# A convolution and a gated layer on one core: each half of a product, copy and sum placed by itself

## Chip, core and metric

The kernel runs on one core of a Trainium2 chip. The metric is the device time of one execution in microseconds (us), the median of several runs. All data are float32; the weights of the layer come as float64 and are turned into float32 by the kernel itself.

## What is computed

A lightweight convolution (each of 8 groups of 24 channels has 7 taps, made by a softmax), then a layer with a sigmoid gate:

```python
# x (8, 4096, 192), weight (8, 7), w_in (192, 2048), w_out (2048, 192)
w = softmax(weight, axis=-1)
conv[b, s, head] = sum_k w[head, k] * x_pad[b, s + k, head]   # causal, 6 zeros ahead
h = conv.reshape(32768, 192) @ w_in
g = h * (1 / (1 + exp(-1.702 * h)))
out = g @ w_out
```

## The kernel before

**Steps.** The 32768 tokens are cut into 32 steps ("big") of 1024: 512 tokens of each of two sequences. The arrays are multiplied by schemes in the manner of Strassen: fewer products of blocks, paid with sums of blocks before and after. Step 0 is done plainly, beside the conversion of the weights; step 1 has its own order; steps 2 to 31 run through the same tables.

**First part of a step** (h = conv @ w_in, and the gate). 20 products (TERMS), each in two rounds (v = 0, 1: two halves of the hidden units), 40 in all. A product has two halves, h = 0 and 1: half 0 takes the rows 0 to 63 of TensorE's array, half 1 the rows 64 to 127, each a matmul of 64x128 weights (w_in_s) on 512 columns of the convolved input (conv_t), each into its own PSUM bank (product1, the matmul is line 598). Products add up in PSUM tiles a0 to a8; between them ScalarE copies a tile to SBUF or to another tile (copy2, L633 and L635 with a sign), VectorE adds or subtracts tiles (sum2, L639), and ScalarE makes the gelus into g (L615 from PSUM, L620 from SBUF). All results that another product adds to must be read first: product 19 adds to a4 only when a5 has been copied from it. In before, `do` issues an item for both halves at once: product half 0, half 1; copy half 0, half 1; sum half 0, half 1.

**Second part of a step** (out = g @ w_out). 78 "main" pieces and 78 "side" matmuls. A main piece is three matmuls of 128x32 weights (w_form, w_out_s) on 256 columns, one in each of three groups of 32 array columns; a side matmul takes the fourth group. `go` issues a main piece and then one side matmul, always in this turn (L855), and the copy of a finished side result (L880). VectorE joins results (L355, L357), transposes the outputs (L771), SyncE stores them. Sums of blocks of g (L355, L357 too, and the accumulating DMAs of POOL, L831) run alongside.

**What prepares the next steps.** Taps of the convolution (ScalarE, L483), their adds (POOL, L501), accumulating DMAs (POOL, L506), sums of conv_t (POOL, L355), SyncE's transfers that put blocks on the other half of the partitions ("cross", L526), loads of x and their transposes (VectorE, L438).

**What sets the order.** All engines take their instructions in the order in which the program issues them, and wait for each other by semaphores. That order is written by hand in tables: ORDER for the first part, PLAN for the second, OPENING for step 0 and step 1, with queues (`todo`, `ready`, `adds`, `tree`, `pieces`) from which "tap", "add", "vsum" and "cross" take the next piece of preparation.

Of the kernel before, what the change touches and what calls it, by code (L numbers as in the profile page):

```python
# [15 lines left out]
def kernel(  # L16
# [38 lines left out]
    xt_pool = ctx.enter_context(tc.tile_pool(name="xt", bufs=1))  # L55
# [6 lines left out]
    xts = {}  # L62
# [103 lines left out]
    def side(big, other, b):  # L166
        return cross_of(big, b) if other else slot_of(big, b)
# [20 lines left out]
    def form(i):  # L188
# [8 lines left out]
    COPY_O = [  # L197
        [(10, 2), (16, 1), (17, 0), (18, 0), (8, 7), (9, 5), (11, 3, -1), (12, 6, -1)],
        [(13, 3), (14, 3), (15, 0), (19, 4), (20, 4), (21, 5), (22, 7)],
        [],  # L200
        [(23, 1), (24, 1), (1, 14), (7, 0, -1)],
    ]
    SUMS_O = [
# [4 lines left out]
    ]  # L208
    TURN_O = (9, 17, 20, 21)

# [105 lines left out]
    def split_rest(i, part=slice(0, PIECE)):  # L316

        lo, hi, m, e = words(i, part)
        ef = e.bitcast(F32)
        act.activation(ef, e, AF.Relu, bias=bias[:, 0:1], scale=-1.0)  # L320
        act.activation(e, ef, AF.Relu, bias=bias[:, 1:2], scale=-(2.0**23))
# [43 lines left out]
    w_left = list(SUMS_W)  # L365

    def next_w(n):
        for _ in range(n):
            add_up(lambda j: w_in_s[:, j, :], *w_left.pop(0))

# [6 lines left out]
    def round_o(i):  # L377
# [15 lines left out]
        round_piece(NW + i, dsts)  # L393

    def add_forms(stage):
        for dst, src, *sign in COPY_O[stage]:
            if sign:
                act.mul(form(dst), form(src), -1.0)
            else:
                act.copy(form(dst), form(src))  # L400
        for dst, src in SUMS_O[stage]:
            nc.gpsimd.dma_start(out=form(dst), in_=form(src), accum_op=ALU.add)

    def end_forms():
        for i in TURN_O:
            act.mul(form(i), form(i), -1.0)
# [26 lines left out]

    def transpose_x(big, c, n=None):
        if big not in xts:
            xts[big] = xt_pool.tile([P, NC, 2, XT], F32, name="xt")
        ns = slice(0, 2) if n is None else slice(n, n + 1)
        vec.transpose(  # L438
            xts[big][:, c, ns, :].rearrange("p n (j t) -> p (n j) t", t=Q),
            xin[:, ns, :, :].rearrange("p n j d -> p (n j) d")[:, :, c * R : c * R + Q],  # L440
        )
# [10 lines left out]
    def tap_home(big, c, k):  # L452
        if big == 1:
            return homes_1[c][k - 1]
        if big < 3:
            return (first_taps if c == 0 else taps[3])[k - 1]
        return taps[c][k - 1]

    def conv_src(big, c, k, ns=slice(0, 2)):
        return xts[big][:, c, ns, Q - PAD + k : Q - PAD + k + T]  # L460

    def conv(big, c, k, ns=slice(0, 2), times=vec.tensor_scalar_mul):
        src = conv_src(big, c, k, ns)
        dst = own(big)[:, 2 * c + ns.start : 2 * c + ns.stop, :]
        tap = cw[:, c, k : k + 1]
        if k == 0:
            times(dst, src, tap)
# [5 lines left out]
    DMA_TAPS = (0,)  # L473
    TAPS_IN = (0, 2, 1)
    ADDS_IN = [(1, 6), (2, 5), (2, 6)] + [(c, k) for c in (2, 1) for k in range(1, K) if (c, k) not in ((1, 6), (2, 5), (2, 6))]
    TREE = {2: [(1, 2)], 4: [(3, 4)], 6: [(5, 6), (0, 1), (3, 5), (0, 3)]}
    TREE_1 = {2: {2: [(1, 2)], 4: [(3, 4), (0, 1)], 6: [(5, 6), (0, 3), (0, 5)]}, 0: {2: [(1, 2)], 4: [(3, 4)], 6: [(5, 6)]}}

    def tap(big, c, k):

        dst = own(big)[:, 2 * c : 2 * c + 2, :]
        home = tap_home(big, c, k) if k else dst
        act.mul(home, conv_src(big, c, k), cw[:, c, k : k + 1])  # L483
        if k and c not in DMA_TAPS and big > 1:
            adds.append((ADDS_IN.index((c, k)), dst, home))
            adds.sort(key=lambda a: a[0])
            if big == 2:
                next_add()
            return
        homes = [dst] + [tap_home(big, c, i) for i in range(1, K)]  # L490
        for a, b in (TREE if big > 1 else TREE_1[c]).get(k, ()):
            tree.append((homes[a], homes[b]))
        if big < 3:
            end_taps(2 if big == 2 and k == K - 1 else 0)

    tree, adds = [], []

    def next_add():
        if adds:
            _, dst, home = adds.pop(0)  # L500
            nc.gpsimd.tensor_add(dst, dst, home)  # L501

    def add_taps():
        if tree:
            out, src = tree.pop(0)
            nc.gpsimd.dma_start(out=out, in_=src, accum_op=ALU.add)  # L506

    def add_pair(c, a, b):

        dst = own(1)[:, 2 * c : 2 * c + 2, :]  # L510
        homes = [dst] + [tap_home(1, c, i) for i in range(1, K)]
        vec.tensor_add(homes[a], homes[a], homes[b])

    def end_taps(left=0):
        while len(tree) > left:
            add_taps()
# [13 lines left out]
    def copy_over(b):  # L530

        for o in range(2):
            act.copy(conv_t[halves[1 - o], cross_of(0, b), :], own(0)[halves[o], b, :])

    pieces, sums_left = [], []
    LAST_AT = {s[0]: i for i, s in enumerate(SUMS_C)}
    ENDS = (NBLK, NBLK + 3, NBLK + 6, NB - 2, NB)
    GROUPS = [range(*ends) for ends in zip(ENDS, ENDS[1:])]  # L540

    def cross_piece():
        if pieces:
            cross(*pieces.pop(0))

    def cross_blocks(big):

        bs = list(REST)
        while bs:
            n = 1  # L550
            while n < min(3, len(bs)) and bs[n] == bs[0] + n:
                n += 1
            pieces.append((big, bs[0], bs[0] + n))
            bs = bs[n:]

    def next_sum():
        if sums_left:
            big, i = sums_left.pop(0)
            sums_c(big, *SUMS_C[i])
            for b in GROUPS:  # L560
                if max(LAST_AT[s] for s in b) == i:
                    pieces.append((big, b[0], b[-1] + 1))

    def begin_sums(big):
        sums_left.extend((big, i) for i in range(len(SUMS_C)))

    def prepare(big):

        for k in range(K if big < 3 else 0):
            yield "", 0.76 if k else 0.48, lambda k=k: conv(big, 1, k)  # L570
        yield f"conv {big}", 0.0, lambda: None
        def done():
            need(f"taps {big}")
            while adds:
                next_add()
            if OPEN_SUM:
                sums_c(big, *OPEN_SUM)
            cross(big, OPEN, OPEN + 1)

        yield f"done {big}", 0.0, done  # L580

    def prepare_taps(big):

        order = [(c, k) for c in (0, 2) for k in range(K)]
        if big > 2:
            order = [(c, 0) for c in TAPS_IN] + [(c, k) for c in TAPS_IN for k in range(1, K)]
        for c, k in order:
            yield "", 1.0, lambda c=c, k=k: tap(big, c, k)
        yield f"taps {big}", 0.0, lambda: None

    def product1(slot, a, b, big, v, first=False):
# [3 lines left out]
        for h in range(2):  # L595
# [11 lines left out]
    ALL = slice(0, TOK)  # L607

    def gelu(b, u, v, src, sign=1):
# [3 lines left out]
        if isinstance(src, list):  # L613
            for h in range(2):
                act.activation(  # L615
                    dst[:, :, h, :], src[h].rearrange("p (o t) -> p o t", o=2), AF.Gelu_apprx_sigmoid,
                    scale=float(sign),
                )
        else:
            act.activation(  # L620
                dst.rearrange("p o h t -> p h o t"),
                src.rearrange("p h (o t) -> p h o t", o=2),
                AF.Gelu_apprx_sigmoid,
                scale=float(sign),
            )
# [3 lines left out]

    def copy2(dst, src, sign=1):  # L630
        for h in range(2):
            if sign == 1:
                act.copy(bank(dst, h), bank(src, h))  # L633
            else:
                act.mul(bank(dst, h), bank(src, h), -1.0)  # L635

    def sum2(op, dst, a, b):
        for h in range(2):
            op(*(bank(t, h) for t in (dst, a, b)))  # L639

# [623 lines left out]
```

## Time and profile before

| | us |
|---|---|
| median of 3 runs (2262.1 to 2263.56) | 2262.73 |
| the profiled execution | 2262.78 |
| its span, first to last instruction | 2261.1 |
| granted TensorE clock, mean | 1.000 |
| step 0 and step 1 (to the first product of step 2's first part) | up to 174.4 |
| a step from 3 on: first part, second part | 35.4, 33.9 |

In the profile's rows, PE is TensorE's matmuls, PEld its weight loads, DVE VectorE, ACT ScalarE, POOL GpSimd and SP SyncE. A row of a group or of the timeline has the line of the kernel, the engine, the operation, the tile written and those read (without numbers), shapes, and how many instructions it merges (x157). A row of the timeline starts with its start and length in us and ends in square brackets with the idle time of the engine ahead of it and what ended it. A row of the chain of waits is a stretch of the work that ended last.

### The profile page before, as it was taken

To read this page: it belongs to the slowest core of one execution; us is meant where nothing else is said; L and a number is where in the kernel's file an instruction comes from. 1 tells how busy PE (TensorE), PEld (TensorE's weight loads), DVE (VectorE), ACT (ScalarE), POOL (GpSimd) and SP (SyncE) were. 2 spreads that over 40 slices of the span, in tenths; PEclk is the share of its full clock that TensorE was granted. 3 is DMA by queue.
4 is the path that set the end of the run, shared out by engine and by line. 5 is a ranking of instruction groups with operands and counts; after the bars stand their busy time and mean duration, and the time that the engine had idled before them with its cause. 6 is when DMAs were issued, how large, how long until landed. Compare 5 with 4: busy or idle time off the path is not lost.

```text
span 2261.1 us, 62136 instructions
## 1 busy us (share of the span) xinstructions
PE 2248.2 (99%) x24966; PEld 1552.0 (69%) x24966; DVE 1985.3 (88%) x2970; ACT 1707.7 (76%) x3233; POOL 1063.9 (47%) x1098
## 2 busy tenths in 40 slices
PE   9999999999999999999999999999999999999999
PEld 5366567766777766777667776667776677766775
DVE  8998888988889888889888898888988888988888
ACT  8677877777777778777787777787777877777754
POOL 1545544455543555444555445554355544455510
PEclk9999999999999999999999999999999999999999
DMA  8986657766667666576565776666866657765543
GB/s 198 174 158 133 125 114 150 143 128 127 121 131 159 128 128 126 111 160 140 125 132 114 141 152 128 129 124 118 163 134 128 124 114 151 144 127 103 104 92 71
DMA packets 275679, 298.05 MB, mean 132 GB/s; under 512 B 119104, under 2 KB 203328, under 8 KB 275392
## 3 DMA queue, kind: packets, MB, share of 16 engines
q0 software_dynamic: 57648, 150.69, 37.0%
q1 hardware_dynamic: 216096, 142.99, 27.8%
q8 instruction: 198, 3.24, 0.6%
q14 instruction: 89, 0.73, 0.1%
q10 hardware_dynamic: 1648, 0.39, 0.1%
HBM read 53.15 MB, written 25.17 MB: 35 GB/s over the span
## 4 chain that ended last, share of the span: by engine, by line
PE 96%; DVE 2%; ACT 1%; issue 1%; DMA 1%; POOL 0%; DVEq 0%; ACTq 0%; POOLq 0%; SPq 0%
PE slot L598 49%; PE slot L855 45%; PE slot L1120 1%; DVE g L357 1%; DMA g<-osbs 0%; PE slot L1115 0%; DVE room L357 0%; ACT g L615 0%; PE slot L946 0%; DVE room L639 0%; ACT w_form L483 0%; DMA xin<-in_x_dram 0%; DVE slot L639 0%; DVE room L355 0%; DVE osbs L771 0%
## 5 line engine op out<-in xcount | busy, mean ns | idle before, releaser
L598 PE MATMUL slot<-conv_t,w_in_s 64*128 64x512 f32 x5152 | 1147.4, 594 | 3.3 <-ACT room L633 1.5
L598 PEld LDWEIGHTS slot<-conv_t,w_in_s 64*128 64x128 f32 x5152 | 663.3, 186 | 474.6 <-issue 312.1
L855 PE MATMUL slot<-g,w_form 128*32 128x256 f32 x9672 | 894.2, 379 | 0.7 <-DVE room L357 0.7
L855 PEld LDWEIGHTS slot<-g,w_form 128*32 128x32 f32 x9672 | 575.6, 110 | 128.9 <-DVE room L357 2.1
L501 POOL TENSOR_TENSOR conv_t<-conv_t,g 128x512 f32<-128x512 f32 x354 | 449.0, 1275 | 88.4 <-ACT g L483 65.4
L855 PE MATMUL slot<-g,w_out_s 128*32 128x256 f32 x5952 | 467.5, 379 | 1.3 <-DVE g L357 0.8
L357 DVE TENSOR_TENSOR g<-g 128x1024 f32<-128x1024 f32 x372 | 450.4, 1224 | 8.0 <-DMA g<-osbs 1.0
L880 ACT COPY room<-slot 32x256 f32<-32x256 f32 x651 | 237.2, 364 | 289.8 <-PE slot L855 281.5
L639 DVE TENSOR_TENSOR room<-slot,room 128x512 f32<-128x512 f32 x620 | 383.6, 679 | 67.8 <-PE slot L598 67.8
L633 ACT COPY room<-slot 128x512 f32<-128x512 f32 x620 | 337.7, 595 | 77.7 <-PE slot L598 61.7
L483 ACT ACTIVATE g<-xt,cw 128x512 f32<-128x512 f32 x534 | 353.9, 715 | 3.7
L620 ACT ACTIVATE g<-room 128x1024 f32<-128x1024 f32 x248 | 265.7, 1071 | 79.0 <-DVE room L639 49.3
L615 ACT ACTIVATE g<-slot 128x512 f32<-128x512 f32 x528 | 282.5, 610 | 51.9 <-PE slot L598 32.8
L831 POOL DMA_DIRECT2D g<-g x124 | 128.1, 1038 | 355.0 <-PE slot L855 330.8
L639 DVE TENSOR_TENSOR slot<-slot,room 128x512 f32<-128x512 f32 x372 | 239.7, 689 | 53.8 <-PE slot L598 52.2
L855 PEld LDWEIGHTS slot<-g,w_out_s 128*32 128x32 f32 x5952 | 239.7, 110 | 43.2 <-DVE room L639 23.3
L355 POOL TENSOR_TENSOR conv_t<-conv_t 128x256 f32<-128x256 f32 x210 | 179.3, 860 | 129.2 <-PE slot L598 119.6
L855 PE MATMUL slot<-osbs,w_form 128*32 128x256 f32 x2232 | 229.5, 379 | 0.0
L506 POOL DMA_DIRECT2D g<-g x120 | 105.9, 883 | 238.1 <-ACT g L483 99.4
L855 PEld LDWEIGHTS slot<-osbs,w_form 128*32 128x32 f32 x2232 | 132.5, 110 | 23.6
L639 DVE TENSOR_TENSOR slot<-room,slot 128x512 f32<-128x512 f32 x124 | 79.8, 687 | 41.8 <-PE slot L598 41.8
L855 PE MATMUL slot<-room,w_form 128*32 128x256 f32 x1488 | 112.9, 379 | 0.0
(166 smaller groups left out, 1662.6 us busy)
## 6 DMA issues: line engine op xcount, KB each, us to landing
g<-g POOLq DMA_DIRECT2D x124, 512.0 KB, 6.5
xin<-in_x_dram SPq DMA_DIRECT2D x240, 180.0 KB, 4.2
conv_t<-conv_t SPq DMA_DIRECT2D x186, 192.0 KB, 5.4
g<-g POOLq DMA_DIRECT2D x120, 256.0 KB, 5.4
conv_t<-conv_t SPq DMA_DIRECT2D x186, 128.0 KB, 2.9
out_dram<-osbs SPq DMA_DIRECT2D x186, 128.0 KB, 2.7
g<-room POOLq DMA_DIRECT2D x31, 512.0 KB, 5.1
conv_t<-g POOLq DMA_DIRECT2D x60, 256.0 KB, 5.4
```

The source lines that it names most:

```text
L355: eng.tensor_add(v(dst), v(a), v(b))
L357: eng.tensor_sub(v(dst), v(a), v(b))
L483: act.mul(home, conv_src(big, c, k), cw[:, c, k : k + 1])
L501: nc.gpsimd.tensor_add(dst, dst, home)
L598: nc.tensor.matmul(slot[h], w_in_s[halves[h], a, v * P : (v + 1) * P], src, start=first, stop=True, skip_group_check=True,)
L615: act.activation(dst[:, :, h, :], src[h].rearrange("p (o t) -> p o t", o=2), AF.Gelu_apprx_sigmoid, scale=float(sign),)
L620: act.activation(dst.rearrange("p o h t -> p h o t"), src.rearrange("p h (o t) -> p h o t", o=2), AF.Gelu_apprx_sigmoid, scale=float(sign),)
L633: act.copy(bank(dst, h), bank(src, h))
L639: op(*(bank(t, h) for t in (dst, a, b)))
L831: nc.gpsimd.dma_start(out=spot(dst), in_=spot(a), accum_op=ALU.add)
L855: nc.tensor.matmul(dst, w, t, start=first, stop=last, skip_group_check=True)
L880: act.copy(to, d)
```

## The change

The amount of work on each engine is unchanged: the same 12483 matmuls, 3230 instructions of ScalarE, 2970 of VectorE, the same DMAs; of the last step's stores one moves from ScalarE's queue to SyncE's. Only the order changes, and with it the waits (semaphore instructions: PE 727 to 582, DVE 1380 to 1344, ACT 906 to 794, POOL 660 to 543, SP 302 to 414).

- `do` takes one half of a product, copy or sum (the last entry of an item; None for both).
- ORDER, PLAN and the queues of preparation are gone. A table STEP, run for the steps 2 to 30, names each instruction or half at its place; LAST does so for step 31.
- In the second part "m" i is main piece i, "s" i side matmul i and "t" i the copy of a finished side result. They stand one by one and no longer strictly in turn; two side tiles have changed places.
- OPENING (steps 0 and 1) is written as such a table too, with the conversion of the weights (split, clip, join, sign, round) cut into its single instructions.

```diff
-    def product1(slot, a, b, big, v, first=False):
+    def product1(slot, a, b, big, v, first=False, hs=range(2)):
...
-        for h in range(2):
+        for h in hs:
...
-        def go(n):
-            for _ in range(n):
-                w, t = now["steps"].pop(0)
-                for c in range(NC):
-                    one_matmul(chunk(now["to"], c), w[:, chunk_cols(c)], t, now["first"], not now["steps"])
-                now["first"] = False
-                d, ws, ts, st, to = side.pop(0)
-                one_matmul(d, ws, ts, st, to is not False)
-                if to is not False:
-                    act.copy(to, d)
...
+        h = args[-1]
+        hs = [h] if h is not None else []
+        if kind == "prod":
+            t, dst, _ = args
+            product1(at(dst), *TERMS[t], big, v, (half, dst, h) not in begun, hs)
...
+    def main_part(i):
+        dst, w, t, first, last = now["todo"][i]
+        for c in range(NC):
+            one_matmul(chunk(dst, c), w[:, chunk_cols(c)], t, first, last)
+
+    def side_part(i):
+        d, w, t, first, to = now["aside"][i]
+        one_matmul(d, w, t, first, to is not False)
...
-    for big in range(1, N_BIG):
...
-            first_products(big, (half, begin_half(), ahead), ORDER)
...
+    for big in range(2, N_BIG - 1):
+        run(STEP, big)
```

Three places show how the order moves.

TensorE in the first part, round 0, around the products 10 and 19. Each row is one half of a product; before, an even and the next odd bank are halves 0 and 1 of one tile. Before, in pairs: products 18 (into a2, slot_73 and slot_74), 10 (a4, slot_69 and slot_70), 17 (a1), 19 (a4), 11 (a1):

```order
L598 MATMUL slot_73<-conv_t,w_in_s 128x512
L598 MATMUL slot_74<-conv_t,w_in_s 128x512
L598 MATMUL slot_69<-conv_t,w_in_s 128x512
L598 MATMUL slot_70<-conv_t,w_in_s 128x512
L598 MATMUL slot_67<-conv_t,w_in_s 128x512
L598 MATMUL slot_68<-conv_t,w_in_s 128x512
L598 MATMUL slot_69<-conv_t,w_in_s 128x512
L598 MATMUL slot_70<-conv_t,w_in_s 128x512
L598 MATMUL slot_67<-conv_t,w_in_s 128x512
L598 MATMUL slot_68<-conv_t,w_in_s 128x512
```

After: a4 is slot_66 (half 0) and slot_67 (half 1), a2 slot_70 and slot_71, a1 slot_64 and slot_65.

```order
L481 MATMUL slot_66<-conv_t,w_in_s 128x512
L481 MATMUL slot_71<-conv_t,w_in_s 128x512
L481 MATMUL slot_67<-conv_t,w_in_s 128x512
L481 MATMUL slot_70<-conv_t,w_in_s 128x512
L481 MATMUL slot_65<-conv_t,w_in_s 128x512
L481 MATMUL slot_64<-conv_t,w_in_s 128x512
L481 MATMUL slot_66<-conv_t,w_in_s 128x512
L481 MATMUL slot_67<-conv_t,w_in_s 128x512
```

Half 0 now goes 10, 18, 17, 19 and half 1 goes 18, 10, 11, 19: product 10 of half 0 stands a product earlier than that of half 1, and ScalarE's two copies a5 <- a4 follow one product apart.

TensorE at the start of the second part. "x3" is a main piece, a single row or "x2" are side matmuls. Before:

```order
L855 MATMUL slot_67<-g,w_out_s 32x256 x3
L855 MATMUL slot_68<-g,w_form 32x256
L855 MATMUL slot_67<-g,w_out_s 32x256 x3
L855 MATMUL slot_68<-g,w_form 32x256
L855 MATMUL slot_67<-g,w_out_s 32x256 x3
L855 MATMUL slot_68<-g,w_form 32x256
```

After:

```order
L741 MATMUL slot_67<-g,w_form 32x256 x2
L741 MATMUL slot_64<-g,w_out_s 32x256 x6
L741 MATMUL slot_65<-g,w_form 32x256 x2
L741 MATMUL slot_64<-g,w_out_s 32x256 x3
L741 MATMUL slot_64<-g,w_form 32x256 x3
L741 MATMUL slot_64<-g,w_out_s 32x256 x3
L741 MATMUL slot_71<-g,w_form 32x256 x2
```

Two side matmuls stand ahead of the first main pieces, and main pieces of different sums (slot_64 with w_out_s or w_form) alternate.

VectorE where step 1 begins. L639 (after: L343) with room and a slot is the sum k0 of step 1, the rows on w_in_s are sums of the weights, L771 (after: L514) turns outputs of step 0. Before:

```order
L771 STREAM_TRANSPOSE osbs<-conv_t 96x16x32
L355 TENSOR_TENSOR w_in_s<-w_in_s 128x256
L357 TENSOR_TENSOR w_in_s<-w_in_s 128x256
L1192 TENSOR_TENSOR room<-room,slot_68 96x512
L357 TENSOR_TENSOR w_in_s<-w_in_s 128x256
L771 STREAM_TRANSPOSE osbs<-slot_70 96x16x32
L771 STREAM_TRANSPOSE osbs<-room 96x16x32
L639 TENSOR_TENSOR room<-slot_73,room 128x512
L639 TENSOR_TENSOR room<-slot_74,room 128x512
```

After:

```order
L343 TENSOR_TENSOR conv_t<-conv_t 128x256 x2
L341 TENSOR_TENSOR conv_t<-conv_t 128x256
L514 STREAM_TRANSPOSE osbs<-slot_67 96x16x32
L1149 TENSOR_TENSOR room<-room,slot_65 96x512
L343 TENSOR_TENSOR room<-slot_70,room 128x512
L343 TENSOR_TENSOR room<-slot_71,room 128x512
L343 TENSOR_TENSOR slot_70<-slot_64,room 128x512
```

The last transpose (osbs<-room) and two sums of weights, which stood ahead of k0, stand behind it.

More of the change, by code (lines that the diff above doesn't have):

```diff
@@ L471, in conv, with add_tap, tree, pair @@
             )
[L473 to L477, printed above, removed]
-    def tap(big, c, k):
[L481 to L516, printed above, removed]
+    def tap(big, c, k):
+        act.mul(tap_home(big, c, k), conv_src(big, c, k), cw[:, c, k : k + 1])
+    def add_tap(big, c, k):
+        nc.gpsimd.tensor_add(tap_home(big, c, 0), tap_home(big, c, 0), tap_home(big, c, k))
+    def tree(big, c, a, b):
+        nc.gpsimd.dma_start(out=tap_home(big, c, a), in_=tap_home(big, c, b), accum_op=ALU.add)
+    def pair(big, c, a, b):
+        vec.tensor_add(tap_home(big, c, a), tap_home(big, c, a), tap_home(big, c, b))
     def sums_c(big, dst, a, op, b):
@@ L528, in cross, with copy_over @@
             )
[L530 to L589, printed above, removed]
-    def product1(slot, a, b, big, v, first=False):
+    def copy_over(b, o):
+        act.copy(conv_t[halves[1 - o], cross_of(0, b), :], own(0)[halves[o], b, :])
+    def product1(slot, a, b, big, v, first=False, hs=range(2)):
         s, c = slot_of(big, b), cross_of(big, b)
@@ L828, in sum_g @@
[L828 to L858 removed]
+    def sum_g(dst, a, op, b):
+        add_up(spot, dst, a, op, b)
@@ L1131, in first_step, with main0, side0 @@
         }
+        aside(
+            (sums[0], sums[1], c11),
+            (listed(s1, t1, (0,)), None, True), (listed(s1, t1, (1,)), p5, False), (p3[:6], q12, False),
+        )
+        def main0(name, what, i, first, stop):
+            w, t = steps[what][i]
+            for c in range(NC):
+                one_matmul(chunk(banks[name], c), w[:, chunk_cols(c)], t, bool(first), bool(stop))
+        def side0(i):
+            dst, w, t, start, to = side[i]
+            one_matmul(dst, w, t, start, to is not False)
```

640 lines of the change are left out of this document (260 added, 380 removed), and 399 rows, old and new, of tables (LAST, MAINS, OPENING, ORDER).

## Prediction

> **What bounds the kernel now.** I read the busy shares and the chain of waits first, to find the engine that sets the end.
>
> ```profile
> PE 2248.2 (99%) x24966; PEld 1552.0 (69%) x24966; DVE 1985.3 (88%) x2970; ACT 1707.7 (76%) x3233; POOL 1063.9 (47%) x1098
> PE 96%; DVE 2%; ACT 1%; issue 1%; DMA 1%; POOL 0%; DVEq 0%; ACTq 0%; POOLq 0%; SPq 0%
> ```
>
> TensorE carries 96% of the chain. Its busy share of 99% tells little, since the rows of matmuls overlap: the question is whether it could go through the same matmuls faster. So I took the chain in order of time, which cuts a step into its two parts (start, length, line).
>
> ```profile
> 243.81 35.42 PE slot L598 x157
> ...
> 382.69 35.41 PE slot L598 x157
> 418.10 33.94 PE slot L855 x624
> ...
> 2186.62 35.07 PE slot L598 x153
> 2221.70 33.88 PE slot L855 x624
> ```
>
> A step from 2 on takes about 35.41 + 33.94 = 69.35 us. Against that stands the beat at which TensorE goes when nothing holds it. Two rows of weight loads in the first part, then rows of matmuls in the second part of the same step:
>
> ```profile
> 384.44 0.19 PEld L598 LDWEIGHTS slot<-conv_t,w_in_s 64*128 64x128 f32 x2 [0.23 <-issue]
> 384.87 0.19 PEld L598 LDWEIGHTS slot<-conv_t,w_in_s 64*128 64x128 f32 x2 [0.24 <-issue]
> ```
>
> ```profile
> 418.03 0.42 PE L855 MATMUL slot<-g,w_out_s 128*32 128x256 f32 x3
> 418.21 0.38 PE L855 MATMUL slot<-g,w_form 128*32 128x256 f32 x1
> 418.27 0.39 PE L855 MATMUL slot<-g,w_out_s 128*32 128x256 f32 x3
> ...
> 451.51 0.39 PE L855 MATMUL slot<-g,w_out_s 128*32 128x256 f32 x3
> ```
>
> A matmul leaves two records (24966 for 12483 matmuls): it is two passes. In the first part the two halves of a product lie on different rows of the array and run side by side, a pair each 0.43 us; 40 products are 80 pairs, 80 x 0.43 = 34.40. In the second part three chunks and one side matmul run side by side; from 418.27 to 451.51 are 154 beats, 33.24 / 154 = 0.216; 78 x 2 x 0.216 = 33.67. Floor of a step: 68.07. The step's other 1.28 us are change-overs (451.51 plus one beat is 451.73, and the next step's first pass starts at 451.97: 0.24; the first beat at 418.03 is 0.24 long, 0.02 too much; some 0.11 more at the first pass of a step, an estimate: about 0.37) and **about 0.91 us of waits**. Who causes them is in the waits of one step (382.69 to 452.04):
>
> ```profile
> PEld slot L598 <- issue: 9.9, 49, 0.4
> PEld slot L855 <- DVE room L639: 0.8, 1, 0.8
> PEld slot L598 <- ACT room L633: 0.6, 2, 0.4
> PEld slot L598 <- ACT slot L635: 0.6, 3, 0.2
> PEld slot L598 <- DVE slot L639: 0.5, 2, 0.3
> ```
>
> "issue" is the normal pause between loads. The other four sum to 2.5 us (two small ones, 0.6, are left out); they hold a pause too, and often stop one half while the other goes on, so the step loses less. All but the one on L855 are of the first part, on copies (L633, L635) and sums (L639) between the PSUM tiles of products. Everything else is covered in a step:
>
> ```profile
> 382.69:452.04 69.35, 69.35 (x786) 49.51 (x786) 60.95 (x91) 53.49 (x102) 34.67 (x36) 1.00 0.65 132
> ```
>
> VectorE works 60.95 and ScalarE 53.49 of 69.35 us, at a granted clock of 1.00. So the waits are of order, not of load.
>
> **The change: steps 2 to 31.** No instruction of an engine goes or comes but waits: the same products, copies, sums, transposes and DMAs. What changes is that each half of a product, copy or sum has a place of its own. The four places where the halves lose, by the loads that came late:
>
> ```profile
> 385.88 0.46 PEld L598 LDWEIGHTS slot<-conv_t,w_in_s 64*128 64x128 f32 x2 [0.39 <-ACT room L633]
> 386.37 0.18 PEld L598 LDWEIGHTS slot<-conv_t,w_in_s 64*128 64x128 f32 x1
> ...
> 393.93 0.29 PEld L598 LDWEIGHTS slot<-conv_t,w_in_s 64*128 64x128 f32 x2 [0.40 <-POOL conv_t L501]
> 394.40 0.29 PEld L598 LDWEIGHTS slot<-conv_t,w_in_s 64*128 64x128 f32 x3 [0.18 <-ACT slot L635]
> ...
> 411.23 0.29 PEld L598 LDWEIGHTS slot<-conv_t,w_in_s 64*128 64x128 f32 x2 [0.20 <-ACT slot L635]
> ...
> 416.98 0.29 PEld L598 LDWEIGHTS slot<-conv_t,w_in_s 64*128 64x128 f32 x2 [0.30 <-DVE slot L639]
> ```
>
> Following the starts of a half's passes through the part, each gap beyond 0.43 is a loss of the slower half: 0.31 at 386 (product 14 behind copy k4), 0.27 at 394 (product 19 behind copy a5), 0.14 at 411 (the same in round 1), 0.17 at 417 (product 13 behind sum a7). Together 0.89, which agrees with the 0.91 above.
>
> The place at 394, worked out: product 19 adds to a4 after a5 was copied from it (L635).
>
> ```profile
> 393.28 1.07 ACT L635 ACTIVATE slot<-slot 128x512 f32<-128x512 f32 x2 [0.25 <-PE slot L598]
> L598 PE MATMUL slot<-conv_t,w_in_s 64*128 64x512 f32 x5152 | 1147.4, 594 | 3.3 <-ACT room L633 1.5
> L639 DVE TENSOR_TENSOR slot<-slot,room 128x512 f32<-128x512 f32 x372 | 239.7, 689 | 53.8 <-PE slot L598 52.2
> ```
>
> Let the last pass of product 10 start at s. Its result is there at s + 0.59 (594 ns a pass). The two halves' copies take 1.07 together, 0.58 each at a pitch of 0.49, so the second half is copied at s + 1.66. Between stands one product, 17, two passes: product 19 could start at s + 0.43 + 0.86 = 1.29. The second half is up to 0.37 late; 0.27 of it is lost, since that half was behind already. After the change half 0 has products 18 and 17 between (needed at s + 2.15, copied at s + 1.17). Half 1 has only product 11 between, but half 0's copy was started a product earlier and no longer stands in front: copied at s + 1.17, needed at 1.29. Not late.
>
> I did the same sum for every copy, sum and gelu that a product of either half waits for, with the medians of the rows (copy 0.58, sum 0.69 by its group above). It finds the four places of before late. In the new order four others come out late: 0.13 at one product in the middle and 0.02 to 0.03 at three, some 0.2. I take 0.15 of it as lost. **Gain 0.90 - 0.15 = 0.75 us a step, 30 steps: -22.5.** Ends: nothing, if new waits stand where the old ones did, and 30 x 0.91 = -27.3, if none is left. I choose near the second end, because the count finds the cause of each old wait gone.
>
> What else is moved: SyncE's cross-over transfers, loads of x and stores, and POOL's adds and accumulating DMAs stand elsewhere in queues that are their own.
>
> ```profile
> conv_t<-conv_t SPq DMA_DIRECT2D x186, 192.0 KB, 5.4
> ```
>
> With landings of this kind (5.4 us for the largest that a product waits for) each still lands over 4 us ahead of its reader. That costs 0; if this cover failed, the price would be a transfer's rest of a few us a step. The second part's pieces are no longer three chunks and one side matmul in turn: the lanes get up to two matmuls apart. I cost that at nothing too (see the first rival). Step 31 has its own table with the same pieces; behind its last matmul all is as before, 0, bounds +-0.3.
>
> **The change: opening.** The rows are busy times by window (length; PE, PEld, DVE, ACT, POOL; clock, DMA share, GB/s): step 0, then step 1's two parts.
>
> ```profile
> 18.60:56.20 37.60, 37.21 (x175) 16.56 (x176) 36.07 (x71) 31.64 (x52) 2.72 (x3) 1.00 0.83 192
> 56.20:101.00 44.80, 43.21 (x356) 13.01 (x356) 44.21 (x76) 25.20 (x48) 21.86 (x24) 1.00 0.94 166
> 101.00:135.00 34.00, 32.83 (x141) 22.96 (x142) 32.05 (x45) 30.56 (x55) 23.35 (x22) 1.00 0.88 166
> 135.00:174.40 39.40, 37.73 (x638) 24.14 (x636) 36.74 (x53) 26.65 (x55) 12.01 (x15) 1.00 0.81 157
> ```
>
> Here VectorE is the bound, and its work is the same after. In step 0 it idles 1.53 + 0.59 = 2.1 us, in step 1 1.95 + 2.66 = 4.6: no order gains more than 6.7 here. Where step 1 begins, the sum k0 stands 1.1 us further ahead in VectorE's queue (two weights' sums and a transpose, 0.37 to 0.66 each, go behind it):
>
> ```profile
> 99.05 0.66 DVE L771 STREAM_TRANSPOSE osbs<-room 96x512 f32<-96x512 f32 x1
> 99.64 1.24 DVE L639 TENSOR_TENSOR room<-slot,room 128x512 f32<-128x512 f32 x2
> ```
>
> ```profile
> 101.01 1.55 PE L598 MATMUL slot<-conv_t,w_in_s 64*128 64x512 f32 x4 [0.72 <-ACT room L633]
> ```
>
> TensorE waits 0.72 there. I take 1.1 for k0 and half of step 1's 4.6 for the rest, 2.3, since nothing in the rows tells between its ends 0 and 4.6: **-3.4**, ends 0 and -6.7.
>
> **Sum.** 2262.78 (the profiled execution: span 2261.1 and 1.68 around it; the median shown is 2262.73, so no correction) - 22.5 - 3.4 = 2236.9: **2237**.
>
> **Rivals.**
>
> *The lanes bind each other.* If TensorE starts matmuls in program order, whatever part of the array they use, a side matmul placed early holds the chunks behind it. I counted turns in the new second part: 87 in place of 78 if none may start before the one ahead of it; the first part stays at 40. Price 9 x 2 x 0.216 = 3.9 us a step, 30 steps +117, less the 26 expected: 2237 + 117 = 2354. It decides from a distance of more than one matmul between lanes. Against it stand the last passes of the first part, each row one pass or the three from it on:
>
> ```profile
> 416.49 1.02 PE L598 MATMUL slot<-conv_t,w_in_s 64*128 64x512 f32 x3
> 416.56 1.11 PE L598 MATMUL slot<-conv_t,w_in_s 64*128 64x512 f32 x3
> 416.92 1.18 PE L598 MATMUL slot<-conv_t,w_in_s 64*128 64x512 f32 x3
> 416.99 0.69 PE L598 MATMUL slot<-conv_t,w_in_s 64*128 64x512 f32 x1
> ```
>
> Passes begin at 416.49, 416.56, 416.92, 416.99 and, with the row of 1.18, 417.51. A half's passes are a beat or more apart, so 416.49 and 416.92 are the last product's two in one half, 416.99 and 417.51 its two in the other, and 416.56 is the product before it: a later matmul had begun 0.07 earlier. For the rival: this is a slip of one pass; two whole matmuls are shown nowhere. Chance 0.09.
>
> The Trainium skill, "TensorE: Matmul & The Clock Gate", Part 3, section "What overlaps and what doesn't", states this rule: "MATMULs are pc-monotone in start AND end — strict FIFO, no reordering". By it the time would be that rival's 2354; the trace disagrees at least for the one pass at 416.49.
>
> *Half the gain.* Copies and sums that now stand one by one also queue one by one behind gelus and taps; late ones appear that my medians don't show. Half of 0.75 a step, -11.3, and -1 in the opening: 2250. Chance 0.21.
>
> *New waits for the old ones.* Step and opening as they were, with 0 to -3: about 2260. That the new order does nothing is this case too. For it: VectorE has 8.4 us of idle time in a step, and a late sum shifts all behind it. Chance 0.06.
>
> *Nothing is left.* No waits in the steps, and most of the opening's idle time: 2262.8 - 27.3 - 6 = 2229. Chance 0.17.
>
> *The opening slips.* Its loads, cross-overs and accumulating transfers stand in a new order on queues that are nearly full (DMA share 0.94 in the second window). If landings there come behind their readers one after another, six of 5.4 us make 32 us, more than the steps give: 2270. Against it: TensorE's and VectorE's busy times there leave little of the windows that a DMA ended. Chance 0.03.
>
> **How the numbers follow.** Forecast 2237: 0.44. Faster is forecast, half the gain and nothing left: 0.82. A measurement here tells about 0.2% (4.5 us) from no change: same 0.06, slower 0.12. The range leaves out the cases of both slower rivals and of no change (0.18) and holds the rest: from a little under 2229, 2226, to a little over 2250, 2254.
>
> **What would show it.** In the chain, L481 rows of 34.6 to 34.8 us per first part and L741 rows of 33.8 to 34.0: sum 68.6. In a step's waits, the copies (L535, L537) and sums (L341, L343) down from 2.5 us in all to under 1. The beats 0.43 and 0.216 as before. If L741 rows stand at 37 to 38, the lanes bind each other. If L481 stays at 35.2 or more, the count of late places is wrong. The start of step 2, now 174.4, should lie near 171. A DMA named as releaser of a load inside a step would make the forecast wrong from the side that I cost at nothing.

## The result and the profile after

The changed kernel takes 2233.88 us (median of 4 runs, 2233.79 to 2234.45) against 2262.51 before (4 runs, 2262.10 to 2263.56): ratio 0.9873, 95% interval 0.9856 to 0.989. The span of the profiled execution fell from 2261.1 to 2232.7, by 28.4 us. The forecast was 2237. Of all executions told of below one was slow, the fourth of the kernel with k0 put back (8841 us at a granted clock of 0.42), and its median leaves it out.

The page's busy shares and chain of waits, after:

```profile
PE 2223.2 (100%) x24966; PEld 1392.3 (62%) x24966; DVE 1987.3 (89%) x2970; ACT 1720.9 (77%) x3233; POOL 1081.4 (48%) x1098
PE 97%; DVE 2%; DMA 1%; issue 0%; ACT 0%; DVEq 0%; POOL 0%; POOLq 0%; ACTq 0%
```

```profile
167.35 34.80 PE slot L481 x159
202.14 33.84 PE slot L741 x624
...
373.24 34.80 PE slot L481 x160
408.04 33.83 PE slot L741 x624
```

The counts of instructions are those of before, and the busy times of VectorE, ScalarE and POOL too, within 2%; that of the weight loads fell by a tenth. TensorE is still the chain. A step takes 34.80 + 33.83 = 68.63 in place of 69.35: 0.61 less in the first part, 0.11 in the second. In a step's first part the gaps between passes beyond 0.43 now make 0.28 in the slower half, where they made 0.89. Step 2 starts (first pass) at 167.28, before at 172.90, 5.6 earlier; from there to the end it is 2065.4 against 2088.2, 22.8 less. Of these the steps 3 to 30 give 19.5, 0.70 each; step 2 gives 2.2 (70.84 to 68.64) and step 31 with the end 1.0. (The 174.4 of the prediction is the edge of a window, not this start.)

The place worked out in the prediction, product 19 of round 0. ScalarE's copies a5 <- a4 and TensorE's loads, after:

```profile
451.64 0.58 ACT L537 ACTIVATE slot<-slot 128x512 f32<-128x512 f32 x1 [1.18 <-PE slot L481]
452.44 0.58 ACT L537 ACTIVATE slot<-slot 128x512 f32<-128x512 f32 x1 [0.22 <-PE slot L481]
...
453.08 0.29 PEld L481 LDWEIGHTS slot<-conv_t,w_in_s 64*128 64x128 f32 x3 [0.22 <-ACT slot L537]
```

Before, one row held both copies (1.07, x2). Now they stand 0.80 apart, the second waits for nothing but its own product, and its reader loads 0.06 after it ends; the half loses 0.08 there in place of 0.27 (by the prediction's working it would lose nothing).

The waits of the loads in one step (304.61 to 373.24), after:

```profile
PEld slot L481 <- issue: 9.7, 45, 0.4
PEld slot L481 <- DVE slot L343: 1.3, 4, 0.6
PEld slot L481 <- DVE room L343: 1.0, 2, 0.5
PEld slot L481 <- ACT room L535: 0.9, 2, 0.6
PEld slot L741 <- ACT g L498: 0.8, 1, 0.8
```

They have **grown**, from 2.5 to 4.0 us (3.2 on copies and sums, 0.8 on a gelu), while the step became shorter. A load that waits while its half still has a pass running delays nothing; only the starts of passes tell what is lost.

The opening by windows (us; busy of PE, PEld, DVE, ACT, POOL; clock, DMA share, GB/s): step 1's first part, its second part, and all up to step 2's first pass. Three rows of before, then three of after.

```profile
94.76:136.80 42.04, 38.87 (x160) 25.25 (x160) 40.09 (x60) 35.24 (x62) 25.17 (x24) 1.00 0.92 171
136.80:172.90 36.10, 34.93 (x625) 22.97 (x625) 33.63 (x46) 24.92 (x52) 11.60 (x14) 1.00 0.79 154
0.00:172.90 172.90, 166.22 (x1451) 88.03 (x1451) 160.48 (x272) 127.00 (x242) 62.64 (x78) 1.00 0.88 175
```

```profile
93.18:131.81 38.63, 37.48 (x164) 21.32 (x160) 36.28 (x54) 32.72 (x57) 26.41 (x26) 1.00 0.90 172
131.81:167.28 35.47, 34.76 (x627) 23.93 (x625) 31.90 (x46) 25.50 (x53) 13.25 (x15) 1.00 0.91 175
0.00:167.28 167.28, 163.04 (x1451) 96.59 (x1451) 155.54 (x272) 127.12 (x242) 64.40 (x79) 1.00 0.90 180
```

Step 0 gives 1.6 us, step 1's first part 3.4, its second part 0.6. The windows of step 1 alone don't hold the same instructions (60 of VectorE's in the one, 54 in the other), so I read VectorE in the last rows: for the same 272 instructions its idle time is 12.4 before and 11.7 after, its busy time 160.5 and 155.5. What fell is the busy time, by 4.9 of the 5.6. Ten other kernels below with the same opening start step 2 between 166.2 and 168.0, so the 5.6 is known to about 1 us at best.

### The profile page after: what moved, and what is told of

Read it like the earlier page. It is cut to its first block, busy times and chain, and to the rows that moved or that the text cites. A ratio compares the mean times of both kernels' runs of the same rounds, so it can differ in the third digit from the quotient of the medians.

```text
span 2232.7 us, 61838 instructions
## 1 busy us (share of the span) xinstructions
PE 2223.2 (100%) x24966; PEld 1392.3 (62%) x24966; DVE 1987.3 (89%) x2970; ACT 1720.9 (77%) x3233; POOL 1081.4 (48%) x1098
## 4 chain that ended last, share of the span: by engine, by line
PE 97%; DVE 2%; DMA 1%; issue 0%; ACT 0%; DVEq 0%; POOL 0%; POOLq 0%; ACTq 0%
PE slot L481 50%; PE slot L741 47%; DMA w_out_s<-w_form 0%; PE slot L795 0%; DVE g L1141 0%; DVE w_in_s L343 0%; DVE room L343 0%; DVE xt L405 0%; DMA w_form<-w_out_s 0%; DVE slot L343 0%; PE slot L387 0%; DVE room L341 0%; DVE osbs L514 0%; DVE osbs L1110 0%; DVE osbs L343 0%
## 5 line engine op out<-in xcount | busy, mean ns | idle before, releaser
L741 PE MATMUL slot<-g,w_form 128*32 128x256 f32 x9672 | 969.0, 379 | 0.0
L481 PEld LDWEIGHTS slot<-conv_t,w_in_s 64*128 64x128 f32 x5152 | 624.4, 186 | 490.4 <-issue 283.1
L741 PEld LDWEIGHTS slot<-g,w_form 128*32 128x32 f32 x9672 | 551.7, 110 | 254.2 <-ACT g L498 22.7
L535 ACT COPY room<-slot 128x512 f32<-128x512 f32 (+1 forms) x806 | 410.2, 540 | 227.5 <-PE slot L741 135.9
L741 PE MATMUL slot<-g,w_out_s 128*32 128x256 f32 (+1 forms) x6048 | 531.7, 383 | 0.0
L343 DVE TENSOR_TENSOR g<-g 128x1024 f32<-128x1024 f32 x372 | 441.5, 1220 | 2.4 <-issue 0.3
L343 DVE TENSOR_TENSOR room<-slot,room 128x512 f32<-128x512 f32 x620 | 362.2, 626 | 13.2 <-PE slot L481 1.0
L741 PE MATMUL slot<-osbs,w_form 128*32 128x256 f32 x2232 | 303.0, 379 | 0.0
L341 POOL TENSOR_TENSOR conv_t<-conv_t 128x256 f32<-128x256 f32 x210 | 206.8, 997 | 172.7 <-PE slot L481 86.2
L343 DVE TENSOR_TENSOR slot<-slot,room 128x512 f32<-128x512 f32 x248 | 163.4, 692 | 8.7 <-PE slot L481 6.6
L341 DVE TENSOR_TENSOR slot<-slot,room 128x512 f32<-128x512 f32 (+1 forms) x155 | 93.9, 642 | 77.4 <-PE slot L481 39.0
L341 DVE TENSOR_TENSOR room<-slot,room 128x512 f32<-128x512 f32 (+1 forms) x248 | 137.3, 554 | 26.1 <-PE slot L481 11.3
```

Of the source, the lines that this page charges most:

```text
L341: eng.tensor_add(v(dst), v(a), v(b))
L343: eng.tensor_sub(v(dst), v(a), v(b))
L481: nc.tensor.matmul(slot[h], w_in_s[halves[h], a, v * P : (v + 1) * P], src, start=first, stop=True, skip_group_check=True,)
L535: act.copy(dst, src)
L741: nc.tensor.matmul(dst, w, t, start=first, stop=last, skip_group_check=True)
```

## The experiments

All times below are medians; the changed kernel is 2233.9, the kernel before 2262.5 to 2262.9 beside each run. The edits are told in words: `prod 10 h0` is half 0 of product 10, and `...` stands for items that stay as they are.

### Which part of the steps gives the gain

Three kernels keep the new opening and step 31 and take the rows of the steps 2 to 30 from the old tables, half by half in pairs: all of it, the first part alone, the second part alone.

```diff
-    STEP = [first part new, second part new]
+    STEP = [first part old, second part old]   # old steps
+    STEP = [first part old, second part new]   # first part old
+    STEP = [first part new, second part old]   # second part old
```

Old steps. 

> The changed kernel with the old order of the steps 2 to 30 in its table (each half where the old tables put it, side tiles as before); opening and step 31 stay new. Theory (opening and steps gain apart from each other): 29 steps x 0.72 us come back, 2233.9 + 20.9 = 2254.8, first parts of 35.4, second parts of 33.9, step 2 starts at 167.3 as in the changed kernel. Rival (the opening's gain is lost where the old steps follow, or the old step 2 keeps the extra 1.5 us that it took before): 2256 to 2261.

First part old. 

> The changed kernel with only the first part of the steps 2 to 30 in the old order (halves in pairs), second part new. Theory (the halves of copies and sums in pairs hold the products): first part 34.80 back to 35.41, second part stays 33.83, 29 x 0.61 = 17.7, so 2251.6. Rival (the gain needs both parts, since what the first part finds ready is left by the second): 2237 or less with a first part below 35.1, or 2255 and more.

Second part old. 

> The changed kernel with only the second part of the steps 2 to 30 in the old order (three chunks and one side matmul in turn), first part new. Theory: only the second part's 0.11 a step come back, 29 x 0.11 = 3.2, so 2237.1, first part 34.8. Rival (the new second part clears the engines' queues for the first one): first part 35.1 and more, 2243 to 2252.

A step of each in the chain of waits: old steps, first part old, second part old.

```profile
446.32 35.40 PE slot L481 x157
481.73 33.94 PE slot L1118 x624
```

```profile
445.88 35.70 PE slot L481 x157
481.58 33.83 PE slot L1118 x624
```

```profile
444.58 35.11 PE slot L481 x159
479.69 34.06 PE slot L1118 x624
```

| kernel | us | ratio to before (95%) | first part | second part | step |
|---|---|---|---|---|---|
| before | 2262.7 | | 35.41 | 33.94 | 69.35 |
| old steps | 2256.93 | 0.9976 (0.9966 to 0.9986) | 35.40 | 33.94 | 69.34 |
| first part old | 2259.46 | 0.9986 (0.9976 to 0.9995) | 35.70 | 33.83 | 69.53 |
| second part old | 2248.78 | 0.994 (0.9925 to 0.9955) | 35.11 | 34.06 | 69.17 |
| changed | 2233.88 | 0.9873 (0.9856 to 0.989) | 34.80 | 33.83 | 68.63 |

With the old steps the old 69.34 is back to a hundredth: the steps' gain is one of order alone, 2256.9 - 2233.9 = 23.0, and the opening and step 31 together are worth 5.7 (2262.7 - 2256.9). Step 2 takes 70.7 there, and took 70.8 before, against 68.6 in the changed kernel; that is the clause that the rival named, 2.1 of the 23.0, and the time lies in the rival's range.

But my theory for the other two fell. Expected were 2251.6 and 2237.1; measured 2259.5 and 2248.8, both in the rivals' ranges. The new second part under an old first part makes the step 0.18 longer than before, the new first part over an old second part gains 0.18, both together gain 0.72. **The gain isn't a sum over the parts.**

### One place undone, and the same place alone

Round 0, products 18, 10, 17, 19 and their copies in pairs again, in the changed kernel:

```diff
-  prod 10 h0, copy a5 h0, prod 18 h1, prod 10 h1, copy a5 h1, prod 18 h0, ..., prod 11 h1, prod 17 h0, prod 19 h0, prod 19 h1
+  prod 18 h0 h1, prod 10 h0 h1, ..., copy a5 h0 h1, copy k6 h0 h1, prod 17 h0 h1, prod 19 h0 h1, prod 11 h1
```

> The changed kernel with one place of round 0 undone in the steps 2 to 30: products 18, 10, 17, 19 with the copies into a5 and k6, halves in pairs again. Theory (two copies back to back with one product between cost the second half 0.27): 29 x 0.27 = 7.8, so 2241.7, the loss visible at product 19, about 11 us into the first part. Rival (another slack takes it up, the waits of a half don't add): 2234 to 2236.

In that kernel the sum k5 of half 1 stood behind the copy that puts k6 into the buffer of k1, and read k6 in place of k1: it computes something else, and its 2342.31 says nothing of the place. With k5 ahead of the copy:

> The changed kernel with one place of round 0 undone in the steps 2 to 30: products 18, 10, 17, 19 and the copies into a5 and k6 with their halves in pairs. Theory (two copies back to back with one product between hold the second half; with no earlier loss that sets the halves apart, the whole 0.37 of the sum shows): 0.3 to 0.4 a step, 29 steps, 2243 to 2246, the loss visible about 11 us into the first part. Rival (the waits of a half are taken up by slack elsewhere): below 0.1 a step, 2234 to 2237.

Measured 2248.24 (0.9935, 0.9918 to 0.9951), first part 35.24. ScalarE and the loads there:

```profile
454.44 1.07 ACT L537 ACTIVATE slot<-slot 128x512 f32<-128x512 f32 x2 [2.04 <-PE slot L481]
...
455.07 0.29 PEld L481 LDWEIGHTS slot<-conv_t,w_in_s 64*128 64x128 f32 x2 [0.69 <-ACT slot L537]
455.56 0.29 PEld L481 LDWEIGHTS slot<-conv_t,w_in_s 64*128 64x128 f32 x3 [0.20 <-ACT slot L537]
```

The two copies stand in one row again, the load of half 1 comes 0.49 behind that of half 0, and that half loses 0.56 there. The step takes 0.50 longer, 0.44 of it in the first part: more than the 0.3 to 0.4 of the theory and its 2243 to 2246, and far from the rival. The mechanism stands, and the place costs more here than the 0.27 of before, as the theory said of halves that no earlier loss has set apart; why 0.56 and not 0.37, no run shows.

The reverse: old steps, and only this place done as in the change, in both rounds.

```diff
-  prod 18 h0 h1, gelu a3, prod 10 h0 h1, gelu k3, prod 17 h0 h1, copy a5 h0 h1, copy k6 h0 h1, prod 19 h0 h1, prod 11 h0 h1
+  gelu a3, prod 10 h0, copy a5 h0, prod 18 h1, prod 10 h1, copy a5 h1, prod 18 h0, copy k6 h0 h1, prod 11 h1, prod 17 h0, prod 19 h0 h1, gelu k3, prod 17 h1, prod 11 h0
```

> The kernel of the run with the old steps (2256.9), and in it one place done as in the change, in both rounds: products 10, 18, 11, 17, 19 with their halves apart, each copy into a5 right behind its half of product 10. Theory (the two halves' copies collide, and that is local): the 0.27 and 0.14 that the old order loses there go, 29 steps x 0.4, about 2245. Rival 1 (the next late copy or sum takes most of it): 2251 to 2257. Rival 2 (an order fits as a whole, and one place changed puts VectorE's or ScalarE's work elsewhere out of step): 2258 and more.

This is round 0. Not in the cut: a transpose of x by VectorE (round 0) and the sum (1, 7) of g, two sums of POOL and an accumulating transfer (round 1) went behind the place too, so the run changes more than the place.

Measured 2266.72 (1.0017, 1.0008 to 1.0027): slower than the old steps by 9.8. The chain's rows are

```profile
377.24 35.74 PE slot L481 x158
412.98 33.98 PE slot L1118 x624
```

The place itself behaves: at product 19 of round 0 the slower half loses 0.13 in place of 0.26. But 0.2 is lost in one half some 9 us into the part and 0.29 at 18 us, where the old order lost 0.03 at most, and the stretch from 26 to 30 us loses 0.3 where it lost 0.14. The time is what rival 2 forecast. Whether the new order of the halves or the pieces that went behind it cost this, the run does not separate.

### Two waits followed to where they go

In the kernel with the first part old, a VectorE sum of g moved behind the sum a6:

```diff
-  gsum(1, 7, "-", 6), ..., sum a6 h0, sum a6 h1
+  ..., sum a6 h0, sum a6 h1, gsum(1, 7, "-", 6)
```

> The kernel of the run with the first part old and the second new (2259.5), and in it one VectorE sum of blocks of g, (1, 7), moved from ahead of product 17 of round 1 to behind the sum a6. There this sum took 1.75 us, beside POOL's additions, where it takes 1.21 elsewhere, and a6 came 0.26 late, with 0.4 lost at product 8 of round 1. Theory (the hybrid loses by this collision): 0.3 a step come back, 29 steps, about 2251. Rival (the pairs lose there by themselves): 2258 to 2260.

Measured 2262.41 (0.9998, 0.9989 to 1.0007), 3 us more. The loss at product 8 of round 1 is gone, as the theory said, and another stands 2 us later:

```profile
547.68 1.22 DVE L343 TENSOR_TENSOR osbs<-osbs,g 128x1024 f32<-128x1024 f32 x1
548.83 1.29 DVE L341 TENSOR_TENSOR slot<-slot,room 128x512 f32<-128x512 f32 x2
...
549.57 0.29 PEld L481 LDWEIGHTS slot<-conv_t,w_in_s 64*128 64x128 f32 x2 [0.49 <-DVE slot L341]
550.17 0.29 PEld L481 LDWEIGHTS slot<-conv_t,w_in_s 64*128 64x128 f32 x2 [0.30 <-DVE slot L341]
```

Sums of g now run right up to the sum a7 (L341), and product 13 waits for a7. The 1.2 us have to stand somewhere in VectorE's queue.

In the kernel with the old steps, the last three taps moved ahead of the last side copies:

```diff
-  ..., copy of side result 20, ..., tap, tap, tap, end of the step
+  tap, main 66, ..., tap, main 70, ..., tap, main 73, ..., copy of side result 20
```

> The kernel of the run with the old steps (2256.9), and in it the last three taps of a step moved from behind the last piece of the second part to pieces 66, 70 and 73. Theory (ScalarE's three taps, 1.95 us, stand ahead of copy k4 and cost the 0.31 at product 14; but halves that a loss has set apart collide less at product 19, where 0.1 comes back): 0.2 a step, 29 steps, 2251. Rival 1 (losses add): 0.31 a step, 2248. Rival 2 (the taps don't hold the copy): 2256 to 2257.

Measured 2295.04 (1.0142, 1.0127 to 1.0157), 38 us slower. ScalarE and the loads where a step begins (449.4):

```profile
448.65 1.33 ACT L444 ACTIVATE g<-xt,cw 128x512 f32<-128x512 f32 x2
450.00 0.37 ACT L1153 COPY room<-slot 32x256 f32<-32x256 f32 x1
450.39 1.07 ACT L535 COPY room<-slot 128x512 f32<-128x512 f32 x2
...
450.42 0.29 PEld L481 LDWEIGHTS slot<-conv_t,w_in_s 64*128 64x128 f32 x2 [0.76 <-ACT room L1153]
451.03 0.29 PEld L481 LDWEIGHTS slot<-conv_t,w_in_s 64*128 64x128 f32 x2 [0.31 <-ACT room L535]
```

Two taps (1.33) now stand ahead of a side copy and of the seed copy k8 (L535, 1.07), on which the step's first products wait; the first part grows to 36.8. With the old steps the seed copies start at 445.42, ahead of the step's first pass at 446.25, and the three taps only at 446.91, while the first products run.

### A buffer exchanged

```diff
-    ROOM_OF = (..., (0, 1, 4, 2, 3, 3, 2, 3, 3, 2))
+    ROOM_OF = (..., (0, 1, 3, 2, 4, 4, 2, 3, 3, 2))
```

> The changed kernel with the buffers of three kept blocks of round 1 exchanged (k4 and k5 in room 4, k2 in room 3), from step 2 on. The copies k4 of round 1 wait for the sum k0, since k8 lies where k4 goes; after the exchange they wait for k9 of round 0, one VectorE sum earlier. Theory (this wait is the 0.1 that both halves lose about 20 us into the first part): 0.05 to 0.1 a step, 30 steps, 2231 to 2232.5. Rival (the products there wait for k0 anyway): 2233.5 to 2234.5.

Measured 2233.47 (0.987, 0.9855 to 0.9884), the step 68.63 as before, and the 0.08 and 0.1 at 20 us of the part unchanged. The wait for a buffer wasn't what held the products there; what did, no run shows. Against the changed kernel this is no difference that can be told.

### How far the lanes of the array may slip

A lane is here a group of array columns (second part) or a half of its rows (first part). The start of the changed kernel's second part shows a whole matmul ahead of one that was issued before it:

```profile
407.97 0.40 PE L741 MATMUL slot<-g,w_form 128*32 128x256 f32 x1
407.99 0.42 PE L741 MATMUL slot<-g,w_out_s 128*32 128x256 f32 x3
408.21 0.38 PE L741 MATMUL slot<-g,w_form 128*32 128x256 f32 x1
...
408.43 0.38 PE L741 MATMUL slot<-g,w_form 128*32 128x256 f32 x1
```

Two side matmuls (w_form) are issued ahead of the first main piece (w_out_s). The first side matmul's passes start at 407.97 and 408.21, the second's at 408.43; the main piece starts at 407.99, 0.44 ahead of the second side matmul. So across lanes TensorE does not start matmuls in the order of issue. The passes at 416.49 and 416.56 in the prediction don't show that yet: the earlier of those two matmuls had begun its first pass at 416.13.

```profile
416.13 1.02 PE L598 MATMUL slot<-conv_t,w_in_s 64*128 64x512 f32 x3
```

How far this goes: the side matmuls held back and issued by four, or by twelve:

```diff
-  s, s, m, m, s, s, m, m, m, ... # at most two matmuls apart
+  m, m, m, s, s, s, s, m, ...    # by four; by twelve: m x 12, s x 12
```

> The changed kernel with the side matmuls of the second part held back and issued four at a time (they lag behind the main pieces by up to 5, and by 2 at most before). By strict program order the second part would need 121 turns in place of 78, 18.6 us a step, 540 in all. Theory (a lane of the array goes on by itself as far as the queue lets it): second part 33.8 to 34.2, 2234 to 2245, side results come up to 1.3 us later. Rival (only a slip of two matmuls is free): a second part longer by 1 us and more, over 2263.

> The same with the side matmuls issued twelve at a time, a lag of up to 13 main pieces. By strict program order 137 turns, 25 us a step, 740 in all. Theory (lanes go by themselves): side results up to 5 us late, at most 2 us a step from joins that wait, below 2295. Rival (the queue holds so many pieces ahead that the side lane runs dry, and the main lanes after it): several us a step, 2300 to 2900.

Measured 2481.18 (1.0963, 1.0947 to 1.098) and 2836.42 (1.2534, 1.2515 to 1.2552). By four: a first part from 475.19, the next from 552.41; by twelve: a second part from 469.83, the next first part from 524.51.

```profile
475.19 34.85 PE slot L481 x160
...
517.29 25.45 PE slot L1118 x386
...
552.41 32.29 PE slot L481 x148
```

```profile
469.83 44.00 PE slot L1118 x493
...
524.51 34.79 PE slot L481 x160
```

The second part takes 552.41 - 475.19 - 34.85 = 42.4 us by four and 54.7 by twelve; the first part is as in the changed kernel. Both theories of mine fell here, and the rivals' side holds: the lanes bind each other once they are far enough apart. The chain of waits in these parts is TensorE's own: by four, the copy of a side result takes 0.4 us of it, by twelve nothing else stands in it. In turns of 0.432 (the two passes of a matmul): 98 and 127, against 78 in the changed kernel.

| counted turns of a second part | before | changed | by four | by twelve |
|---|---|---|---|---|
| strict program order | 78 | 87 | 121 | 137 |
| a lane may run 2 passes ahead of its own last start | 78 | 78.5 | 105.5 | 128.5 |
| 3 passes | 78 | 78 | 92 | 122 |
| measured | 78 | 78 | 98 | 127 |

In the table a pass may be put into its lane as soon as the pass two (or three) before it in the same lane has started, and all passes are put in by program order. The measured times lie between the rows of two and three. So the new order's slips, two matmuls at most, just fit: 78.5 turns by the first rule, 78 by the second. The rules are fitted to these four orders; no run between a lag of two and one of five was made.

### The opening: k0

```diff
-  sum k0 h0, ..., sum k0 h1, ..., w_in 19, ..., turn(0, 1, q12), ..., w_in 23
+  w_in 19, w_in 23, turn(0, 1, q12), sum k0 h0, ..., sum k0 h1
```

> The changed kernel with two sums of weights and one transpose of step 0 put back ahead of the sum k0 where step 1 begins, as in the old order. Theory of the prediction (k0's place in VectorE's queue is worth 1.1): 2235.0, step 2 starts 1.1 us later than at 167.3. Rival (VectorE is busy all through step 1, and what stands first there doesn't count): 2233.9, step 2 starts within 0.3 of 167.3.

Measured 2236.01 (three runs, 2235.88 to 2236.18; 0.988, 0.986 to 0.99), 2.1 more. Step 2 starts at 167.51, 0.2 later than in the changed kernel, as the rival said; but the chain shows step 2's first part at 35.41 in place of 34.80. The chain's row and the loads there:

```profile
167.58 35.41 PE slot L481 x158
...
167.51 0.29 PEld L481 LDWEIGHTS slot<-conv_t,w_in_s 64*128 64x128 f32 x2 [0.41 <-issue]
167.99 0.72 PEld L481 LDWEIGHTS slot<-conv_t,w_in_s 64*128 64x128 f32 x5 [0.19 <-DMA conv_t<-conv_t]
```

Half 1 of step 2's first product starts 0.48 after half 0, in the changed kernel 0.06, and its load waits for a cross-over transfer. That is most of the 0.6. Whether k0's place made that transfer late, one profile doesn't tell: in four other kernels with the changed kernel's opening half 1 starts 0.01 to 0.23 after half 0. Step 31 starts 1.3 later. The three runs all lie above the changed kernel's four, so the move may be worth about 2 us, but the intervals overlap, and the loss does not lie where I put it.

## Why the prediction was right, and where not

1. **Bound and floor**: right. The beats 0.43 and 0.216 stayed, the step went to 68.63, 0.19 over the floor with its change-overs (68.44); 68.6 was forecast.
2. **Steps, -22.5**: measured -22.8. The cause is shown for one place (product 19 undone: 0.50 a step), and that only order was at work by the old steps, which bring 69.34 back. Right in size, but the way of the sum, waits that go one by one, is wrong: four partial orders (first part, second part, product 19 alone, the sum of g) came out 0.3 to 0.8 a step longer than a sum over places said. The other three late places were not undone one by one. The size is in part luck: the steps 3 to 30 gave 0.70 each in place of 0.75, which is 1.5 short, 0.11 of a step came from the second part, for which I had no term, and step 2 with 2.2 and step 31 with 1.0 made up for it.
3. **Product 19**: 0.37 late by the working, 0.27 lost before, 0.08 lost after (none by the working), 0.56 lost where it alone is undone.
4. **Opening, -3.4**: measured -5.6 by step 2's start, inside the ends 0 and -6.7 but for another reason. I wrote that VectorE's work is the same and took half of its idle time. Its idle time fell by 0.7 only; some of its instructions became shorter (below). The 1.1 for k0 isn't gained in step 1: put back, k0 moves step 2's start by 0.2, less than that start varies from kernel to kernel. The wait of 0.72 that I showed for it names a copy of ScalarE, not k0.
5. **Lanes cost nothing**: right for this order, and in part by luck: the passes that I showed told nothing of whole matmuls, and two matmuls of slip are about the limit. None of the rival's 117 was paid, but its mechanism exists: by four, 20 of the 43 turns that strict order would add are paid, by twelve 49 of 59. The Trainium skill, "TensorE: Matmul & The Clock Gate", Part 3, "What overlaps and what doesn't", has matmuls in strict program order; the changed kernel's 33.83, where that order needs 87 turns or 37.6 us, disagrees, and so do the runs by four and by twelve, at 42.4 and 54.7 where it needs 52.3 and 59.2.
6. **Signs to look for**: first part 34.80, second 33.83, beats: as forecast. The loads' waits, forecast below 1 us, went to 3.2 (4.0 with the gelu): a wrong sign, since most of them hold nothing up.
7. **DMAs at nothing**: no DMA appears as a releaser of a load in the changed kernel's steps. The cover of 4 us was not everywhere there, though: with k0 put back, a transfer holds half of step 2's first product (above).

What stays open: which instruction costs each of the partial orders its 0.3 to 0.8 a step. Two were followed (sums of g ahead of a7; taps ahead of the seed copy), the others only located.

## What to carry to other kernels

Where an engine's two halves wait for copies that run one after the other on a third engine, put different products into the halves so that their copies don't fall together; shift them by a product or so. Keep lanes of the array close in the order of issue: in this second part slips of two matmuls were free, and a lag of up to five cost 8.5 us a step. Judge an order by the starts of passes, not by the waits of weight loads, and try it as a whole: an order half changed can be slower than both.

## What the runs showed of the hardware

**VectorE and POOL take time from each other.** The same VectorE sum of g, 128x1024 from SBUF to SBUF, and POOL's sums of conv_t, by shape, before and then after:

```profile
L357 DVE TENSOR_TENSOR osbs<-osbs,g 128x1024 f32<-128x1024 f32 x31 | 52.2, 1685 | 0.0
L355 POOL TENSOR_TENSOR conv_t<-conv_t 128x256 f32<-128x256 f32 x210 | 179.3, 860 | 129.2 <-PE slot L598 119.6 <-DVE conv_t L469 0.4
```

```profile
L343 DVE TENSOR_TENSOR osbs<-osbs,g 128x1024 f32<-128x1024 f32 x31 | 37.8, 1218 | 0.0
L341 POOL TENSOR_TENSOR conv_t<-conv_t 128x256 f32<-128x256 f32 x210 | 206.8, 997 | 172.7 <-PE slot L481 86.2 <-DVE room L343 78.3 <-DVE conv_t L439 3.4
```

Of the 683 VectorE sums of this shape, 592 of before share no time with a POOL addition and take 1.22 (none over 1.23); the 64 that share more than 0.3 us with one are all longer, 1.30 to 2.36. 63 took over 1.35 before, 2 after: in the new order it is POOL's sums that are longer (0.86 to 1.00 us), and POOL isn't on the chain. Much of the opening's gain goes with it: up to step 2's start VectorE's 23 such sums went from 1.33 to 1.24 us on average and its 12 multiply-adds of the convolution (128x512) from 0.93 to 0.82, together 3.4 us of its time. Six of these 35 were clearly longer than the rest before, each beside an addition of POOL, and three after. That this is what moves step 2's start is argued from the sums of time, not tested. The Trainium skill, "SBUF — State Buffer", section "SBUF: two separate sides", says that VectorE and GpSimd share a pair of ports as an exclusive lock; the trace agrees, with 1.22 us alone and up to 2.36 beside an addition of POOL. I did not try a kernel that takes the additions away.
